# A DiT block on one core: the first K steps of the attention input by token tile, scalings by one engine each, plus-one on ScalarE, tile 2 normalized by VectorE

## The chip, the core and the metric

The kernel runs on one core of a Trainium2 chip. A core has a matrix engine (TensorE; in the profile PE, and PEld for its weight loads), VectorE (DVE), ScalarE (ACT), GpSimd (POOL) and SyncE (SP), which here only issues transfers. Each engine works through its own list of instructions in order; across engines an instruction waits on semaphores. The metric is the time of one execution on the device in microseconds (us); lower is better. Before and after are each the median of several runs.

## What is computed

One diffusion-transformer block on 2 x 256 tokens of width D = 1152, in bfloat16:

```python
mod = (_silu(c) @ w_mod).reshape(B, 6, 1, D)
shift_a, scale_a, gate_a, shift_m, scale_m, gate_m = [mod[:, i] for i in range(6)]
h = _layernorm(x, axis=-1) * (1 + scale_a) + shift_a
qkv = (h @ wqkv).reshape(B, N, 3, H, Dh)
...
a = jnp.einsum('bhqk,bkhd->bqhd', attn, v).reshape(B, N, D) @ wo
x = x + gate_a * a
h2 = _layernorm(x, axis=-1) * (1 + scale_m) + shift_m
m = _gelu(h2 @ w_fc1) @ w_fc2
return x + gate_m * m
```

The change lies entirely in the first two steps that use x: the layer norm with its scale, and the K part of `qkv`.

## The kernel before

The 512 tokens are four tiles of 128, numbered 0 to 3; tiles 0 and 1 belong to the first batch entry, 2 and 3 to the second. The width 1152 is nine chunks of 128, called k = 0 to 8. K, Q and V are then computed, followed by attention, the output projection, the second layer norm and the two feed-forward matrix products, all of which are untouched.

The start of the kernel, which the change reorders, works on several strands at once:

- **Statistics.** For tiles 0, 2 and 3 VectorE takes `bn_stats` of three pieces of 384 columns (line 167) and aggregates them (L169). Tile 1's sums come from two passes on ScalarE (L179), finished by three small VectorE operations (L184, L187, L190). ScalarE takes the square root (L195), VectorE the reciprocal (L198).
- **Normalization.** `norm1` writes the normalized tile `xn`, first its columns 0 to 511 (`CUT` is four chunks), later the rest. VectorE does it in one operation from mean and reciprocal (L211). ScalarE can do it too (L206), but then needs the product `nb` of mean and reciprocal (L200). Before, tile 2's first part is on ScalarE, all else on VectorE; `nb` is formed for tiles 0 and 2.
- **The scale.** `scale_group(g)` computes the scale for two or three chunks with 18 or 27 narrow matmuls from `w_scale_a` into a PSUM tile `pm` (L224), and VectorE adds one as it copies it to `scale_a` (L228).
- **Transposing and scaling.** `transpose_x` transposes 128 x 128 blocks of `xn` on TensorE into a PSUM tile `pt` (L234). `modulate` multiplies by the scale and writes the operand `hT0` (the profile calls it big), on VectorE (L241) or ScalarE (L243).
- **K steps.** `k_step(k, c0, c1)` multiplies chunk k of token columns c0 to c1 by six 128-wide weight blocks of `w_k` and adds into six PSUM banks `pk` that stay open over all k (L256). Each reloads the six weight blocks, however many columns it has.

What sets the order: the body is written out by hand, and the last lines of the kernel tie every instruction to the one recorded before it on its engine, so each engine runs exactly in the order of the source. The tiles `pc`, `pm` and `pt` share a pool named aux with two buffers, used in turn; a new one waits until the tile two before it has been read. Weights arrive through SyncE's queue in the fixed order of the source: a group of `w_scale_a`, then the rows of `w_k` for the same chunks, four times over; then the rest of `w_k`, `w_shift_a`, `w_q`, and so on. They are cut so that early chunks come first.

The order before: tile 0 and tile 1 are transposed for chunks 0 and 1 into one shared `pt_0`, the scale group comes between them, ScalarE scales chunk 0 for both tiles and VectorE chunk 1, and K steps 0 and 1 run over 256 token columns. Then tile 2 and tile 3 follow one at a time, with chunks 2 and 3 of the first two tiles in between. Each pair of chunks 2 and 3 is likewise shared between ScalarE and VectorE. A filler `warm(1)` of one matmul on zeros (L150) stands ahead of the first K step.

Of the kernel before, what the change touches and what calls it, by code (L numbers as in the profile page):

```python
# [8 lines left out]
FP32 = mybir.dt.float32  # L9
BF16 = mybir.dt.bfloat16  # L10
ACT = mybir.ActivationFunctionType
# [8 lines left out]
def kernel(  # L20
# [11 lines left out]
    nc = tc.nc  # L32
    B, N, D = x.shape
# [3 lines left out]
    P = 128  # L37
# [7 lines left out]
    NPD = D // PW  # L45
# [6 lines left out]
    const = ctx.enter_context(tc.tile_pool(name="const", bufs=1))  # L52
# [6 lines left out]
    def acc_tile(shape, name, dt=FP32):  # L59
        return psum.tile(shape, dt, name=name, tag="acc", bufs=6)  # L60

    def aux_tile(shape, name, dt=FP32):
        return psum.tile(shape, dt, name=name, tag="aux", bufs=2)
# [26 lines left out]
    make_identity(nc, ident[:])  # L90
    eps_t = const.tile([P, 1], FP32, name="eps_t")
    nc.vector.memset(eps_t[:], LN_EPS)  # L92
    SW = 32
    sT = act.tile([P, KD, SW], BF16, name="sT")
    nc.gpsimd.memset(sT[:], 0.0)
# [49 lines left out]
    pwarm = acc_tile([P, T], "pwarm")  # L145


    def warm(n, dst):
        for _ in range(n):
            nc.tensor.matmul(dst[:], zeros[:, 0:P], zeros[:], start=True, stop=True)  # L150
# [9 lines left out]
    mv1 = small.tile([P, NT, 2], FP32, name="mv1", tag="mv1", bufs=1)  # L160
# [2 lines left out]
    xns = [work.tile([P, D], BF16, name="xn", tag="xn", bufs=4) for _ in range(NT)]  # L163
    stats1 = [small.tile([P, NPD, 6], FP32, name="stats1", tag="stats1") for _ in range(NT)]

    def stats_piece(t, j):
        nc.vector.bn_stats(stats1[t][:, j, :], x_sb[:, t, j * PW:(j + 1) * PW])  # L167
        if j == NPD - 1:
            nc.vector.bn_aggr(mv1[:, t, :], stats1[t][:].rearrange("p a b -> p (a b)"))  # L169


    T_ACT = 1
# [10 lines left out]
    def act_stats_finish():  # L183
        nc.vector.scalar_tensor_tensor(  # L184
            dm2[:], dsum[:], -1.0 / (D * D), dsum[:], op0=ALU.mult, op1=ALU.mult
        )
        nc.vector.scalar_tensor_tensor(  # L187
            mv1[:, T_ACT, 1:2], dsq[:], 1.0 / D, dm2[:], op0=ALU.mult, op1=ALU.add
        )
        nc.vector.scalar_tensor_tensor(  # L190
            mv1[:, T_ACT, 0:1], dsum[:], -1.0 / D, pivot, op0=ALU.mult, op1=ALU.add
        )

    def sqrt1(t):
        nc.scalar.activation(rstd1[:, t:t + 1], mv1[:, t, 1:2], ACT.Sqrt, bias=eps_t[:], scale=1.0)  # L195

    def recip1(t, with_nb=False):
        nc.vector.reciprocal(rstd1[:, t:t + 1], rstd1[:, t:t + 1])  # L198
        if with_nb:
            nc.vector.scalar_tensor_tensor(  # L200
                nb1[:, t:t + 1], mv1[:, t, 0:1], -1.0, rstd1[:, t:t + 1], op0=ALU.mult, op1=ALU.mult
            )

    def norm1(t, c0, c1, eng):
        if eng == "a":
            nc.scalar.activation(  # L206
                xns[t][:, c0:c1], x_sb[:, t, c0:c1], ACT.Identity,
                bias=nb1[:, t:t + 1], scale=rstd1[:, t:t + 1],
            )
        else:  # L210
            nc.vector.tensor_scalar(  # L211
                xns[t][:, c0:c1], x_sb[:, t, c0:c1], mv1[:, t, 0:1], rstd1[:, t:t + 1],
                op0=ALU.subtract, op1=ALU.mult,
            )


    scale_a = act.tile([P, KD, B], FP32, name="scale_a")

    def scale_group(g):
        k0, k1 = KGROUPS[g]  # L220
        pm = aux_tile([P, k1 - k0, B], "pm")
        for j in range(k0, k1):
            for k in range(KD):
                nc.tensor.matmul(  # L224
                    pm[:, j - k0, :], w_scale_a[:, k, j * P:(j + 1) * P], sT[:, k, 0:B],
                    start=(k == 0), stop=(k == KD - 1),
                )
        return lambda: nc.vector.tensor_scalar_add(scale_a[:, k0:k1, :], pm[:], 1.0)  # L228

    def transpose_x(ks, ts, pt=None, js=None):  # L230
        pt = aux_tile([P, len(ks), len(ts) * P], "pt", BF16) if pt is None else pt
        for i, k in enumerate(ks):
            for j, t in enumerate(ts) if js is None else zip(js, ts):
                nc.tensor.transpose(pt[:, i, j * P:(j + 1) * P], xns[t][:, k * P:(k + 1) * P], ident[:])  # L234
        return pt

    def modulate(pt, i, k, t0, j0, w, eng):
        b = t0 // TPB
        dst, src, sc = hT0[:, k, t0 * P:t0 * P + w], pt[:, i, j0:j0 + w], scale_a[:, k, b:b + 1]
        if eng == "d":  # L240
            nc.vector.tensor_scalar_mul(dst, src, sc)  # L241
        else:
            nc.scalar.mul(dst, src, sc)  # L243

    def modulated_transpose(k):
        pt = transpose_x([k], range(NT))
        for b in range(B):
            modulate(pt, 0, k, b * TPB, b * N, N, "da"[k % 2])
# [3 lines left out]
    def k_step(k, c0=0, c1=T):  # L252
        for m in range(KM1):
            if k == 0 and c0 == 0:
                pk[m] = acc_tile([P, T], "pk")
            nc.tensor.matmul(  # L256
                pk[m][:, c0:c1], w_k[:, k, m * P:(m + 1) * P], hT0[:, k, c0:c1],
                start=(k == 0 and c0 == 0), stop=(k == KD - 1), skip_group_check=True,
            )
# [30 lines left out]
    CUT = 4 * P  # L290
    warm(16, pwarm)
    act_stats(ACT.Identity, dsum)
    for j in range(NPD):
        stats_piece(0, j)
    sqrt1(0)
    act_stats(ACT.Square, dsq)
    stats_piece(2, 0)
    recip1(0, True)
    norm1(0, 0, CUT, "d")
    stats_piece(2, 1)  # L300
    pt_0 = aux_tile([P, 2, N], "pt", BF16)
    transpose_x([0, 1], [0], pt_0, [0])
    act_stats_finish()
    sqrt1(T_ACT)
    stats_piece(2, 2)
    recip1(1)
    norm1(1, 0, CUT, "d")
    scale_group(0)()
    transpose_x([0, 1], [1], pt_0, [1])
    modulate(pt_0, 0, 0, 0, 0, N, "a")  # L310
    modulate(pt_0, 1, 1, 0, 0, N, "d")
    sqrt1(2)
    warm(1, pwarm)
    k_step(0, 0, N)
    k_step(1, 0, N)
    stats_piece(3, 0)
    recip1(2, True)
    norm1(2, 0, CUT, "a")
    stats_piece(3, 1)
    stats_piece(3, 2)  # L320
    pt_1 = transpose_x([0, 1], [2])
    for k in range(2):
        modulate(pt_1, k, k, 2, 0, P, "a")
    sqrt1(3)
    scale_group(1)()
    recip1(3)
    pt_2 = transpose_x([2, 3], [0, 1])
    modulate(pt_2, 0, 2, 0, 0, N, "a")
    modulate(pt_2, 1, 3, 0, 0, N, "d")
    norm1(3, 0, CUT, "d")  # L330
    k_step(0, N, N + P)
    k_step(1, N, N + P)
    pt_3 = transpose_x([0, 1], [3])
    for k in range(2):
        modulate(pt_3, k, k, 3, 0, P, "a")
    k_step(2, 0, N)
    k_step(3, 0, N)
    norm1(0, CUT, D, "d")
    norm1(1, CUT, D, "d")
    pt_4 = transpose_x([2, 3], [2, 3])  # L340
    modulate(pt_4, 0, 2, 2, 0, N, "a")
    modulate(pt_4, 1, 3, 2, 0, N, "d")
    norm1(2, CUT, D, "d")
    norm1(3, CUT, D, "d")
    k_step(0, N + P, T)
    k_step(1, N + P, T)
    scale_group(2)()
    k_step(2, N, T)
    modulated_transpose(4)
    k_step(3, N, T)  # L350
    modulated_transpose(5)
    k_step(4)
    scale_group(3)()
    modulated_transpose(6)
    k_step(5)
    modulated_transpose(7)
# [10 lines left out]
    def vec_section(stat, w, name):  # L367
        pn = aux_tile([P, CTW], "pn")
        for k in range(KD):
            wk4 = w[:, k, :].rearrange("p (j q r) -> p q j r", q=4, r=32)  # L370
            for i in range(4):
                nc.tensor.matmul(  # L372
                    pn[32 * i:32 * i + SW, :].rearrange("p (j r) -> p j r", r=32),
                    stat[:, k, :], wk4[:, i, :, :],
# [14 lines left out]
    for k in range(KD):  # L389
        for b in range(B):  # L390
            dst, src = hT[:, k, b * N:(b + 1) * N], hT0[:, k, b * N:(b + 1) * N]
# [37 lines left out]

    s_rows = work.tile([P, KD, SW], BF16, name="s_rows", tag="s_rows", bufs=1)  # L430
    nc.vector.transpose(s_rows[:].rearrange("p k c -> p (k c)"), sT[:].rearrange("p k c -> p (k c)"))
# [301 lines left out]
    for b in range(B):  # L733
        for m0 in range(0, MSPLIT, 2):
# [7 lines left out]
            nc.scalar.activation(gT[:, ms[0]:ms[-1] + 1, b * N:(b + 1) * N], pacc[:], ACT.Gelu_apprx_tanh)  # L742
    gcol = small.tile([P, SW], FP32, name="gcol", tag="gcol", bufs=1)
    nc.gpsimd.memset(gcol[:], 0.0)
    gcol16 = small.tile([P, SW], BF16, name="gcol16", tag="gcol16", bufs=1)
    grow16 = small.tile([P, SW], BF16, name="grow16", tag="grow16", bufs=1)

# [33 lines left out]
    for gi, (n, t, c0, cw) in enumerate(groups):  # L781
        b = t // TPB
        last = gi == len(groups) - 1
        pacc = acc_tile([P, cw], "pacc")
        for kk in range(KF):
            j, r = divmod(n * KF + kk, 27)
# [15 lines left out]
    for ins in list(nc.cur_bb.bb.instructions)[first_traced:]:  # L802
        eng = ins.engine
# [38 lines left out]
```

## Time and profile before

| what | value |
|---|---|
| median of three runs | 245.58 us (245.22 to 245.62) |
| the profiled execution's own time | 245.54 us |
| its span, first to last instruction | 243.7 us |
| granted TensorE clock, mean over the span | 0.997 of full |
| normalization of 512 columns on VectorE (L211), mean | 407 ns |
| the same on ScalarE (L206), mean | 812 ns |
| one `bn_stats` piece on VectorE (L167), mean | 549 ns |
| scaling 256 columns from PSUM on VectorE (L241), mean | 350 ns |
| scaling 256 columns on ScalarE (L243), mean | 474 ns |
| scaling 128 columns on ScalarE (L243), mean | 363 ns |

The means are those of the groups between 7 and 16 us. The profile is one execution; its times count from the first instruction of the span. An engine's busy time is the time its instructions take, whatever depends on them; a wait is put down to the instruction that ended it. TensorE overlaps its matmuls, so a matmul's own length (some 0.2 to 0.4 us) is more than its share of a stream: the distance from start to start is what it costs there. VectorE and ScalarE likewise overlap the ends of neighbouring instructions a little when the second does not wait for the first. A line such as `pt<-ident,xn` names the result and the operands.

### The profile page before, as it was taken

The page shows a single profiled execution, that of the slowest core. Times are in us where ns is not written, and L with a number is a line of the kernel's source. Part 1 is how long each engine was busy: PE and PEld are TensorE (multiplying, and loading weights), DVE is VectorE, ACT ScalarE, POOL GpSimd, SP SyncE. Part 2 cuts the span into 40 slices and gives each one's busy share as a digit, 9 for nine tenths or more (in the row PEclk, how much of TensorE's full clock was granted, in tenths as well). Part 3 has the DMA queues.
Part 4 walks back from the last instruction along what each step waited for, and adds up shares of the span by engine and source line. Part 5 has one row for each costly group of instructions (what it writes and reads, how often), then busy time and mean ns, then how long its engine had stood idle before and what let it go on. Part 6 is the DMA issues. An engine that isn't in the chain of part 4 may idle for free.

```text
span 243.7 us, 3933 instructions
## 1 busy us (share of the span) xinstructions
PE 236.2 (97%) x1659; PEld 141.3 (58%) x1668; DVE 84.2 (35%) x196; ACT 66.2 (27%) x129; POOL 31.4 (13%) x47
## 2 busy tenths in 40 slices
PE   7879999999999999999999999999999999999994
PEld 2476444465656675888744444444666666666673
DVE  2853541314644676820000089993010000000001
ACT  6542250233524074783332222333000000000000
POOL 1000004000310514400000000003122211111111
PEclk9999999999999999999999999999999999999998
DMA  6999999999989977779999999996920000000000
GB/s 226 328 333 360 384 349 324 359 354 342 346 199 346 344 208 185 193 187 332 327 337 191 233 298 329 328 327 181 310 96 16 19 16 16 16 21 29 18 19 16
DMA packets 69757, 53.89 MB, mean 221 GB/s; under 512 B 19035, under 2 KB 64363, under 8 KB 69739
## 3 DMA queue, kind: packets, MB, share of 16 engines
q1 hardware_dynamic: 69008, 52.43, 72.7%
q0 software_dynamic: 704, 1.20, 1.7%
q8 instruction: 13, 0.21, 0.4%
q14 instruction: 5, 0.04, 0.0%
q10 hardware_dynamic: 27, 0.00, 0.0%
HBM read 48.08 MB, written 1.19 MB: 202 GB/s over the span
## 4 chain that ended last, share of the span: by engine, by line
PE 93%; DVE 3%; DMA 2%; ACT 1%; issue 1%; DVEq 0%
PE pacc L787 29%; PE pacc L726 29%; PE pacc L628 7%; PE pacc L519 7%; PE pacc L446 5%; PE pk L256 4%; PE pk L285 2%; PE pacc L454 2%; DMA x_sb<-in_x_dram 2%; PE pn L372 1%; PE ps_s L474 1%; PE pa L546 1%; DVE stats L167 1%; PE pt L234 1%; PE pm L224 1%
## 5 line engine op out<-in xcount | busy, mean ns | idle before, releaser
L787 PE MATMUL pacc<-w_f,gT 128*128 128x384 bf16 (+2 forms) x468 | 70.5, 314 | 0.0
L726 PE MATMUL pacc<-hT,w_f 128*128 128x512 bf16 (+1 forms) x409 | 70.1, 332 | 0.3
L787 PEld LDWEIGHTS <-gT 128*128 128x128 bf16 x468 | 44.4, 98 | 26.3
L726 PEld LDWEIGHTS <-w_f 128*128 128x128 bf16 x414 | 40.5, 98 | 29.4
L437 DVE SCALAR_TENSOR_TENSOR late<-w_gate_mT,late 128x1152 bf16<-128x1152 bf16 x18 | 24.4, 1357 | 32.7 <-DMA w_gate_mT<-in_w_mod_dram 32.1
L793 DVE TENSOR_TENSOR tmp<-pacc,gate 128x384 f32<-128x384 f32 (+2 forms) x13 | 6.8, 526 | 67.0 <-PE pacc L787 54.8
L764 ACT ACTIVATE gT<-pacc 128x512 bf16<-128x512 f32 x26 | 15.5, 597 | 35.0 <-PE pacc L726 35.0
L795 POOL TENSOR_TENSOR o_sb<-tmp,x 128x384 bf16<-128x384 f32 (+1 forms) x12 | 11.7, 973 | 52.0 <-DVE tmp L793 52.0
L628 PE MATMUL pacc<-w_o,big 128*128 128x384 bf16 (+2 forms) x117 | 18.1, 314 | 0.0
L519 PE MATMUL pacc<-w_v,hT 128*128 128x384 bf16 x108 | 17.9, 326 | 0.0
L628 PEld LDWEIGHTS <-big 128*128 128x128 bf16 x117 | 10.9, 98 | 7.1 <-DVE big L273 0.6
L519 PEld LDWEIGHTS <-hT 128*128 128x128 bf16 x108 | 10.4, 98 | 7.2 <-issue 0.5
L256 PE MATMUL pk<-big,w_k 128*128 128x256 bf16 (+2 forms) x88 | 13.3, 292 | 0.5 <-ACT big L243 0.3
L634 POOL TENSOR_TENSOR x<-tmp,x_sb 128x384 f32<-128x384 f32 (+1 forms) x11 | 9.8, 888 | 19.4 <-DVE tmp L633 10.8
L446 PE MATMUL pacc<-hT,w_q 128*128 128x512 bf16 x53 | 11.8, 379 | 0.1
L428 POOL DMA_DIRECT2D gates_dram<-grow x4 | 2.0, 514 | 66.2 <-DVE grow L750 66.2
L256 PEld LDWEIGHTS <-w_k 128*128 128x128 bf16 x90 | 7.5, 98 | 3.6 <-issue 0.6
L446 PEld LDWEIGHTS <-w_q 128*128 128x128 bf16 x54 | 5.3, 97 | 6.4
L150 PE MATMUL pwarm<-zeros 128*128 128x512 bf16 x21 | 7.6, 524 | 1.2 <-DVE eps_t L92 1.2
L633 DVE TENSOR_TENSOR tmp<-pacc,gate 128x384 f32<-128x384 f32 (+2 forms) x13 | 6.7, 525 | 5.4 <-PE pacc L628 5.3
L742 ACT ACTIVATE gT<-pacc 128x512 bf16<-128x512 f32 x10 | 5.7, 595 | 7.0 <-PE pacc L726 7.0
L611 ACT ACTIVATE hT<-hT,shift_m,scale_m 128x256 bf16<-128x256 bf16 x12 | 6.2, 588 | 4.0 <-DMA hT<-xn 4.0
(98 smaller groups left out, 156.0 us busy)
## 6 DMA issues: line engine op xcount, KB each, us to landing
w_f<-in_w_fc_dram SPq DMA_DIRECT2D x14, 864.0 KB, 10.5
w_f<-in_w_fc_dram SPq DMA_DIRECT2D x2, 2592.0 KB, 10.7
w_f<-in_w_fc_dram SPq DMA_DIRECT2D x2, 1728.0 KB, 12.0
w_shift_a<-in_w_mod_dram SPq DMA_DIRECT2D x3, 864.0 KB, 10.6
w_v<-in_wqkv_dram SPq DMA_DIRECT2D x3, 864.0 KB, 11.3
w_gate_a<-in_w_mod_dram SPq DMA_DIRECT2D x3, 864.0 KB, 9.8
w_o<-in_wo_dram SPq DMA_DIRECT2D x3, 864.0 KB, 13.6
w_shift_m<-in_w_mod_dram SPq DMA_DIRECT2D x3, 864.0 KB, 9.8
```

What stands on the lines that cost most here:

```text
L150: nc.tensor.matmul(dst[:], zeros[:, 0:P], zeros[:], start=True, stop=True)
L256: nc.tensor.matmul(pk[m][:, c0:c1], w_k[:, k, m * P:(m + 1) * P], hT0[:, k, c0:c1], start=(k == 0 and c0 == 0), stop=(k == KD - 1), skip_g ...
L437: nc.vector.scalar_tensor_tensor(spill, wT[:, j, :], 1.0, s_all[:, b, :], op0=ALU.mult, op1=ALU.mult, accum_out=dst[:, b * KD + j:b * KD + ...
L446: nc.tensor.matmul(pq[m][:], w_q[:, k, m * P:(m + 1) * P], hT[:, k, :], start=(k == 0), stop=(k == KD - 1),)
L519: nc.tensor.matmul(pacc[:], hT[:, k, t * P:(t + 1) * P], w_v[:, k, pnl * PW:(pnl + 1) * PW], start=(k == 0), stop=(k == KD - 1),)
L628: nc.tensor.matmul(pacc[:], aT[:, k, t * P:(t + 1) * P], w_o[:, k, c0:c1], start=(k == 0), stop=(k == KD - 1),)
L634: (nc.vector if (t, i) in ((1, 2), (3, 3)) else nc.gpsimd).tensor_tensor(x1[:, t, c0:c1], tmp[:], x_sb[:, t, c0:c1], op=ALU.add)
L726: nc.tensor.matmul(dst, w_f1[m // KD][:, k, ml * P:(ml + 1) * P], hT[:, k, c0:c1], start=(k == 0), stop=(k == KD - 1),)
L764: nc.scalar.activation(gT[:, m, :], pacc[:], ACT.Gelu_apprx_tanh)
L787: nc.tensor.matmul(pacc[:], gT[:, kk, t * P:(t + 1) * P], w_f2[j][:, r, c0 - n * PW:c0 - n * PW + cw], start=(kk == 0), stop=(kk == KF - 1),)
L793: nc.vector.tensor_tensor(tmp[:], pacc[:], gate_m[:, b, c0:c0 + cw], op=ALU.mult)
L795: (nc.vector if last else nc.gpsimd).tensor_tensor(o_sb[:], tmp[:], x1[:, t, c0:c0 + cw], op=ALU.add)
```

## The change

Four things are done, all within the hand-written order of the start.

Tile 1 no longer shares `pt_0` with tile 0. Each is transposed into a PSUM tile of its own, scaled by one engine (tile 0 by ScalarE, tile 1 by VectorE), and K steps 0 and 1 run once over tile 0's 128 columns and once over tile 1's. The later pairs of chunks 2 and 3 are each scaled by ScalarE alone, and tile 3's chunks 0 and 1 by VectorE instead of ScalarE. The filler matmul is dropped.

For scale groups 0 and 1 ScalarE adds the one, with a constant `one_t` as the bias of an identity activation; groups 2 and 3 stay on VectorE.

Tile 2's first part is normalized by VectorE, and the two products `nb` are no longer formed.

The aggregation of tile 2's statistics moves behind the normalization of tile 1, and the plus-one of group 1 before tile 3's square root; tile 3's normalization now stands ahead of the transposes of chunks 2 and 3.

```diff
+    one_t = const.tile([P, 1], FP32, name="one_t")
+    nc.vector.memset(one_t[:], 1.0)
...
-    def stats_piece(t, j):
+    def stats_piece(t, j, aggregate=True):
         nc.vector.bn_stats(stats1[t][:, j, :], x_sb[:, t, j * PW:(j + 1) * PW])
-        if j == NPD - 1:
-            nc.vector.bn_aggr(mv1[:, t, :], stats1[t][:].rearrange("p a b -> p (a b)"))
+        if j == NPD - 1 and aggregate:
+            stats_aggregate(t)
+
+    def stats_aggregate(t):
+        nc.vector.bn_aggr(mv1[:, t, :], stats1[t][:].rearrange("p a b -> p (a b)"))
...
-        return lambda: nc.vector.tensor_scalar_add(scale_a[:, k0:k1, :], pm[:], 1.0)
+
+        def add_one(eng):
+            dst = scale_a[:, k0:k1, :]
+            if eng == "d":
+                nc.vector.tensor_scalar_add(dst, pm[:], 1.0)
+            else:
+                nc.scalar.activation(dst, pm[:], ACT.Identity, bias=one_t[:])
+
+        return add_one
...
-    recip1(0, True)
+    recip1(0)
     norm1(0, 0, CUT, "d")
     stats_piece(2, 1)
-    pt_0 = aux_tile([P, 2, N], "pt", BF16)
-    transpose_x([0, 1], [0], pt_0, [0])
+    pt_0 = transpose_x([0, 1], [0])
     act_stats_finish()
     sqrt1(T_ACT)
-    stats_piece(2, 2)
+    stats_piece(2, 2, False)
     recip1(1)
     norm1(1, 0, CUT, "d")
-    scale_group(0)()
-    transpose_x([0, 1], [1], pt_0, [1])
-    modulate(pt_0, 0, 0, 0, 0, N, "a")
-    modulate(pt_0, 1, 1, 0, 0, N, "d")
+    stats_aggregate(2)
+    scale_group(0)("a")
+    for k in range(2):
+        modulate(pt_0, k, k, 0, 0, P, "a")
+    pt_1 = transpose_x([0, 1], [1])
+    for k in range(2):
+        modulate(pt_1, k, k, 1, 0, P, "d")
     sqrt1(2)
-    warm(1, pwarm)
-    k_step(0, 0, N)
-    k_step(1, 0, N)
+    k_step(0, 0, P)
+    k_step(1, 0, P)
     stats_piece(3, 0)
-    recip1(2, True)
-    norm1(2, 0, CUT, "a")
+    recip1(2)
+    norm1(2, 0, CUT, "d")
+    k_step(0, P, N)
+    k_step(1, P, N)
     stats_piece(3, 1)
     stats_piece(3, 2)
-    pt_1 = transpose_x([0, 1], [2])
+    pt_2 = transpose_x([0, 1], [2])
     for k in range(2):
-        modulate(pt_1, k, k, 2, 0, P, "a")
+        modulate(pt_2, k, k, 2, 0, P, "a")
+    scale_group(1)("a")
     sqrt1(3)
-    scale_group(1)()
     recip1(3)
-    pt_2 = transpose_x([2, 3], [0, 1])
-    modulate(pt_2, 0, 2, 0, 0, N, "a")
-    modulate(pt_2, 1, 3, 0, 0, N, "d")
     norm1(3, 0, CUT, "d")
+    pt_3 = transpose_x([2, 3], [0, 1])
+    for i, k in enumerate((2, 3)):
+        modulate(pt_3, i, k, 0, 0, N, "a")
     k_step(0, N, N + P)
     k_step(1, N, N + P)
-    pt_3 = transpose_x([0, 1], [3])
+    pt_4 = transpose_x([0, 1], [3])
     for k in range(2):
-        modulate(pt_3, k, k, 3, 0, P, "a")
+        modulate(pt_4, k, k, 3, 0, P, "d")
     k_step(2, 0, N)
     k_step(3, 0, N)
     norm1(0, CUT, D, "d")
     norm1(1, CUT, D, "d")
-    pt_4 = transpose_x([2, 3], [2, 3])
-    modulate(pt_4, 0, 2, 2, 0, N, "a")
-    modulate(pt_4, 1, 3, 2, 0, N, "d")
+    pt_5 = transpose_x([2, 3], [2, 3])
+    for i, k in enumerate((2, 3)):
+        modulate(pt_5, i, k, 2, 0, N, "a")
...
-    scale_group(2)()
+    scale_group(2)("d")
...
-    scale_group(3)()
+    scale_group(3)("d")
```

## The prediction, made before the changed kernel was run

> **What bounds the kernel now.** I read the page first, then the chain that ended last, the busy times by stretch, the waits of TensorE, and last the timeline of the stretch that the diff touches.
>
> ```profile
> span 243.7 us, 3933 instructions
> ...
> PE 236.2 (97%) x1659; PEld 141.3 (58%) x1668; DVE 84.2 (35%) x196; ACT 66.2 (27%) x129; POOL 31.4 (13%) x47
> ...
> PE 93%; DVE 3%; DMA 2%; ACT 1%; issue 1%; DVEq 0%
> ```
>
> TensorE carries 93% of the chain. What is not TensorE must lie somewhere, and the stretches say where:
>
> ```profile
> 8.47:15.54 7.07, 4.87 (x76) 3.73 (x75) 4.76 (x19) 3.01 (x8) 0.00 (x0) 1.00 1.14 323
> 15.54:26.72 11.18, 11.07 (x129) 7.87 (x130) 3.48 (x13) 2.78 (x7) 0.00 (x0) 1.00 1.08 364
> 34.92:240.20 205.28, 204.93 (x1370) 123.30 (x1374) 67.66 (x142) 50.81 (x97) 30.39 (x40) 1.00 0.71 206
> ```
>
> Columns are the stretch, its length, busy time of PE, weight loads, VectorE, ScalarE, GpSimd, the granted clock and DMA. From 15.5 us to 240.2 us TensorE is gapless at full clock, so a microsecond saved before 15.5 us is saved at the end, unless a weight lands too late for it. Only 8.5 to 15.5 us has holes, and TensorE's waits name them:
>
> ```profile
> PE pt L234 <- DVE scale_a L228: 0.8, 2, 0.5
> PE pt L234 <- DVE xn L211: 0.6, 1, 0.6
> PE pt L234 <- ACT xn L206: 0.5, 1, 0.5
> PE pk L256 <- ACT big L243: 0.3, 1, 0.3
> ```
>
> The timeline there (start, length, what) gives the present dates and most prices:
>
> ```profile
> 8.73 0.60 PE L224 MATMUL pm<-sT,w_scale_a 128*128 128x2 bf16 x18
> ...
> 10.14 0.47 ACT L243 ACTIVATE big<-pt,scale_a 128x256 bf16<-128x256 bf16 x1 [1.41 <-PE pt L234]
> 10.51 0.28 ACT L195 ACTIVATE rstd<-mv,eps_t 128x1 f32<-128x1 f32 x1
> 10.65 0.35 DVE L241 TENSOR_SCALAR big<-pt,scale_a 128x256 bf16<-128x256 bf16 x1 [0.89 <-ACT big L243]
> ...
> 11.76 0.81 ACT L206 ACTIVATE xn<-x_sb,nb,rstd 128x512 bf16<-128x512 bf16 x1 [0.96 <-DVE nb L200]
> ...
> 12.95 0.62 ACT L243 ACTIVATE big<-pt,scale_a 128x128 bf16<-128x128 bf16 x2 [0.38 <-PE pt L234]
> ...
> 14.52 0.35 DVE L241 TENSOR_SCALAR big<-pt,scale_a 128x256 bf16<-128x256 bf16 x1 [0.57 <-ACT big L243]
> ...
> 15.25 0.29 PE L234 MATMUL pt<-ident,xn 128*128 128x128 bf16 x2 [0.60 <-DVE xn L211]
> ```
>
> To see there: VectorE's scaling waits for ScalarE to leave the shared pair (0.89 and 0.57 us), and the work queued behind it on VectorE, tile 3's normalization among it, waits too. Tile 2's normalization takes 0.81 us on ScalarE, against 0.41 us for the same shape on VectorE (L211).
>
> **What the Trainium skill says.** "PSUM — Partial Sum Buffer", PSUM bank collisions: two engines must not touch one bank at once, so their accesses are put in order. The trace agrees: those 0.89 and 0.57 us. "ScalarE: Activation LUTs", What ACT_TABLE_LOAD costs and Table sets: an ACTIVATE with a per-partition bias costs some 280 ns plus 0.83 ns an element, and cheap functions such as identity are in every table set. The trace agrees with the first (0.28 to 0.29 us for one element, L195); Identity already runs between Sqrts (L179, L206) with no table load between. "TensorE: Matmul & The Clock Gate", Part 1: the clock halves after an idle window of about 3.4 us. The trace has no such gap after the warm-up and a clock of 1.00 in all three stretches.
>
> **The change part by part.** TensorE's prices, start to start: four transposes 0.22 us (16.68 to 16.91), twelve 128-wide K matmuls 0.66 (16.91 to 17.57), eighteen scale matmuls 0.46 (17.57 to 18.03), six 256-wide 0.65 (18.03 to 18.68). A signal to another engine costs 0.03 to 0.05 us. I walk the new order with these.
>
> 1. VectorE's start. The two products nb (L200) go, 0.08 us each on the path (7.12 to 7.20), and tile 2's aggregation (0.23) moves behind tile 1's normalization, which starts at about 8.93 instead of 9.27 and ends at 9.34. I count this gain as nothing: see 2. The new memset of one_t (0.06) lies in VectorE's idle time before 4.81.
>
> 2. Scale group 0 and tile 0. The scale matmuls stay at 8.73 (they waited 0.15 us for w_scale_a) and end at 9.33. Plus-one on ScalarE: not in the trace; the page's price and the Sqrt row agree on 0.29 (VectorE's took 0.15; from above, 0.47, the 256-wide activation): 9.37 to 9.66. Two 128-wide activations, 0.62: 9.70 to 10.32. The "aux" tag has two PSUM buffers: tile 1's transposes now need a buffer of their own, and it is tile 0's, free only when ScalarE has read it. So they start at 10.37, later than the present 9.83, done 0.28 later. VectorE scales both chunks: one 256-wide takes 0.35, two 0.61, so 0.26 per 256 elements beyond a fixed 0.09; two of 128 come to about 0.35: 10.69 to 11.04. VectorE sits idle from 9.5 to 10.69, which is where part 1's gain goes.
>
> 3. K steps 0 and 1 as four half steps: 24 matmuls instead of 12 double ones, 1.32 us against 1.30. Tile 0's start behind the transposes at 10.48; tile 1's are due at 11.14, VectorE done at 11.04. They end at 11.80, against 11.97 before (10.67 plus 1.30). The warm-up matmul (0.21) went from a hole: nothing.
>
> 4. Tile 2. VectorE: first statistics of tile 3 (10.97 to 11.52), reciprocal (11.43 to 11.57; its Sqrt, on ScalarE behind tile 0's scaling, is done at 10.53), normalization 0.41: 11.61 to 12.02. Transposes at 12.07 instead of 12.62: 0.55 gained. Scale group 1 at 12.18; its weights land at 4.5 + 7.3 = 11.8. ScalarE scales tile 2 from 12.39 to 13.01, which frees the buffer for the transposes of chunks 2 and 3: 13.06 instead of 13.59. The plus-one follows (12.94 to 13.23).
>
> 5. Tile 3. VectorE pays 0.41 for tile 2 first, so the other statistics take 11.94 to 12.95 and the aggregation 13.22 (12.93 before). Sqrt 13.26 to 13.55, reciprocal to 13.74, then normalization directly, 13.78 to 14.19, not behind a scaling that waits for ScalarE (14.79 before). Transposes at 14.24 against 15.25: 1.01 gained, the largest piece.
>
> 6. What follows. ScalarE alone scales chunks 2 and 3 (0.84 for two, L243) from 13.49: done 13.96 and 14.33. K step 2 starts at 14.36 (15.37 before), K step 3 at 15.01 (16.01). Row 3 of w_k was issued at 7.57 (4.95 plus the queue's 2.57) and takes 7.4 to land: 14.97. Just in time; a larger gain would stop here. Then 15.66, 15.88, 16.54, 17.00 for the next transposes, tile 3's K steps, scale group 2 and K step 2's second half; ScalarE's two scalings of those transposes (16.07 to 16.91) are ready when used (17.00 and 17.87). From there the old order runs, 1.0 us earlier.
>
> 7. Later weights. w_scale_a's third group lands at 14.8 (due 16.5), the fourth at 18.5 (due 20.1); w_k's last rows by 20.7 (due about 24). w_shift_a's last third lands at 30.5 (18.7 plus 11.8), due about 31.4: 0.9 us to spare. w_q's first piece 32.1, due 33.7. The queue's order is unchanged.
>
> Sum: 1.0 us less. The profiled run took 245.54 us for a span of 243.7, and the median of the runs shown is 245.58: 245.54 - 1.0 = 244.5.
>
> **Rivals.** (a) The ScalarE chain of part 2 is longer. It starts from a transfer's landing at 8.7 and has no slack now: VectorE idles behind it. With the plus-one at 0.47, 0.1 us more for its own wait and a landing 0.2 later, parts 4 to 6 move by 0.5: 245.0. For it: every step is serial. Against: each price is a measured row. (b) Landings take over: with row 3 of w_k 0.9 us later, or the last third of w_shift_a 1.8, only 0.1 us of gain is left: 245.4. For it: w_k has no margin. Against: only row 3 is so near. Landings alone cannot end slower than before, since they would be waited for then too. (c) Slower: TensorE now idles once from 9.2 to 10.37. If the clock fell to half there, the 2.9 us of work until 13.9 (0.11 + 1.32 + 0.11 + 0.46 + 0.22 + 0.66) would take 5.8; the holes of some 0.9 us in that stretch absorb part, and about 2 us more remain: 246.5. It decides once the drop lasts for more than half of that. Against: 1.2 us is far under the stated window, and the trace's clock stood through holes of 0.5 us. (d) More: if landings come early and signals are at the short end, 1.4 us: 244.1.
>
> **How the numbers follow.** Forecast 244.5 with 0.66 (own range 244.1 to 245.0), (a) 0.16, (b) 0.06, (c) 0.06, (d) 0.06. The range 244.0 to 245.3 takes in (a), (d) and the two ends of the plus-one. 0.2%, about what can be told here, is 0.49 us, so the line is 245.09: the forecast, (d) and half of (a) are faster, 0.80; the rest of (a) and (b) are the same, 0.14; (c) slower, 0.06.
>
> **What would show it.** Right: transposes of tiles 1, 2 and 3 at about 10.4, 12.1 and 14.2; tile 1's later than before, the others earlier; K step 3 at 15.0; no hole after it. Wrong: a wait of K step 3 on w_k (b), a plus-one well over 0.3 us or VectorE idle beyond 10.7 (a), 128-wide K matmuls over 0.1 us apart (c).

## The result and the profile after

The changed kernel took 244.1 us (median of six runs, 243.66 to 244.63) beside 245.4 us for the kernel before (six runs, 245.16 to 246.8): a ratio of 0.994, interval 0.9913 to 0.9966. Two later repeats of the unedited changed kernel gave 0.9954 [0.9936, 0.9973] and 0.9935 [0.9907, 0.9963]. The forecast was 244.5 in a range of 244.0 to 245.3: the direction is right and the time lies in the range, 0.3 to 0.4 us under the forecast. Which step of the prediction failed is the question here.

One thing is needed to read sizes this small: in about a third of the runs of the kernel before (77 of the 229 for which it is recorded) the mean granted TensorE clock was 0.993 or less, and 61 of those took over 246.5 us, so each median below is also given for the runs at a clock of 0.997 or more (nothing lies between). On that footing the kernel before takes 245.16 us (152 runs; the middle half 245.12 to 245.34) and the changed one 244.12 (21 runs; 243.95 to 244.23): **1.04 us less**. The profile behind the prediction, at 245.54, sat 0.38 us above the kernel's usual time. The last section returns to the clock.

The page of the changed kernel, first its totals and then the shares of the chain of waits:

```profile
span 242.9 us, 3965 instructions
...
PE 237.0 (98%) x1679; PEld 141.6 (58%) x1679; DVE 84.3 (35%) x195; ACT 66.0 (27%) x131; POOL 31.4 (13%) x47
...
PE 86%; SPq 7%; DMA 5%; issue 0%; DVE 0%; DVEq 0%
```

The busy times of the engines barely move (TensorE's even shows 0.8 us more, with some of its records missing from the earlier profile); the span is 0.8 us shorter. Waits of TensorE in the same run, from 7 us on (us in total, times, longest):

```profile
PE pt L247 <- DVE mv L174: 0.5, 1, 0.5
PE pt L247 <- ACT big L256: 0.3, 1, 0.3
```

None of the four waits shown before is left in the list, and two smaller ones stand in their place. The transposes of tiles 2 and 3 still follow their normalization, but TensorE now stands for only about 0.1 us there. What that bought stands in the timeline of that run (start, length, what, and the idle time ahead with its releaser):

```profile
9.99 0.27 PE L247 MATMUL pt<-ident,xn 128*128 128x128 bf16 x2 [0.47 <-DVE mv L174]
...
11.89 0.28 PE L247 MATMUL pt<-ident,xn 128*128 128x128 bf16 x2
...
14.06 0.29 PE L247 MATMUL pt<-ident,xn 128*128 128x128 bf16 x2
14.18 1.47 PE L269 MATMUL pk<-big,w_k 128*128 128x256 bf16 x12
```

These lines are the transposes of tiles 1, 2 and 3 and the start of K step 2, due by the prediction at 10.37, 12.07, 14.24 and 14.36. All came earlier. Yet this is the slowest of the six runs: the second half of x landed at 6.9 us (6.2 in the profile before), VectorE ran late from there, and later a weight came late. The same stretch of a repeat of the same program that took 243.96 us is the better picture:

```profile
9.28 0.26 ACT L239 ACTIVATE scale_a<-pm,one_t 128x4 f32<-128x4 f32 x1 [0.75 <-PE pm L229]
9.57 0.63 ACT L256 ACTIVATE big<-pt,scale_a 128x128 bf16<-128x128 bf16 x2
9.59 0.27 PE L247 MATMUL pt<-ident,xn 128*128 128x128 bf16 x2 [0.35 <-ACT scale_a L239]
9.98 0.47 DVE L254 TENSOR_SCALAR big<-pt,scale_a 128x128 bf16<-128x128 bf16 x2 [0.58 <-ACT big L256]
...
11.48 0.28 PE L247 MATMUL pt<-ident,xn 128*128 128x128 bf16 x2
...
13.65 0.29 PE L247 MATMUL pt<-ident,xn 128*128 128x128 bf16 x2
13.78 1.47 PE L269 MATMUL pk<-big,w_k 128*128 128x256 bf16 x12
```

The third line is the one to look at. Tile 1's transposes start at 9.59, beside ScalarE's scaling of tile 0 (9.57 to 10.20) and not behind it; what released them was the plus-one. The prediction had them wait for that scaling.

### The profile page after: what moved, and what is told of

It is laid out like the page before. It is cut to its first block, busy times and chain, and to the rows that moved or that the text cites. A ratio compares the mean times of both kernels' runs of the same rounds, so it can differ in the third digit from the quotient of the medians.

```text
span 242.9 us, 3965 instructions
## 1 busy us (share of the span) xinstructions
PE 237.0 (98%) x1679; PEld 141.6 (58%) x1679; DVE 84.3 (35%) x195; ACT 66.0 (27%) x131; POOL 31.4 (13%) x47
## 4 chain that ended last, share of the span: by engine, by line
PE 86%; SPq 7%; DMA 5%; issue 0%; DVE 0%; DVEq 0%
PE pacc L803 29%; PE pacc L742 29%; PE pacc L644 7%; PE pacc L535 7%; DMA w_shift_a<-in_w_mod_dram 5%; PE pacc L462 5%; SPq L109 4%; PE pacc L470 2%; SPq L115 2%; PE pa L562 1%; PE ps_s L490 1%; PE pn L388 1%; PE pk L298 1%; SPq L104 1%; PE pg L422 0%
## 5 line engine op out<-in xcount | busy, mean ns | idle before, releaser
L269 PE MATMUL pk<-big,w_k 128*128 128x128 bf16 (+2 forms) x102 | 13.4, 278 | 0.0
```

Source lines behind the costliest of these rows:

```text
L269: nc.tensor.matmul(pk[m][:, c0:c1], w_k[:, k, m * P:(m + 1) * P], hT0[:, k, c0:c1], start=(k == 0 and c0 == 0), stop=(k == KD - 1), skip_g ...
```

## The experiments

Times are medians in us, with the number of runs; "clock up" means a mean granted clock of 0.997 or more. The ratio is to the kernel before on the same chip, over all runs. Differences below are between medians with the clock up: against 244.12 for edits of the changed kernel and against 245.16 for edits of the kernel before. They are good to some 0.1 to 0.4 us; the kernel before alone has 245.14 to 245.26 on the four chips.

| kernel | median | ratio, interval | median, clock up |
|---|---|---|---|
| before, again | 245.36 (18) | 0.9999 [0.9977, 1.0021] | 245.16 (10) |
| changed, repeats | 244.13 (11), 244.20 (9) | 0.9954 [0.9936, 0.9973], 0.9935 [0.9907, 0.9963] | 244.08 (8), 244.14 (7) |
| changed, tile 1 in tile 0's buffer | 244.95 (22) | 0.9988 [0.9966, 1.0011] | 244.71 (13) |
| changed, scale bank apart | 244.09 (9) | 0.9938 [0.9912, 0.9965] | 243.94 (6) |
| before, pair on ScalarE alone | 244.45 (22) | 0.9969 [0.995, 0.9988] | 244.41 (18) |
| before, tile 2 on VectorE | 244.57 (19) | 0.9949 [0.9932, 0.9966] | 244.57 (17) |
| changed, tile 2 on ScalarE | 244.40 (12) | 0.9965 [0.994, 0.9991] | 244.35 (11) |
| changed, plus-one on VectorE | 244.13 (14) | 0.9938 [0.992, 0.9957] | 244.12 (11) |
| changed, K steps not split | 244.48 (22) | 0.9965 [0.9948, 0.9982] | 244.31 (19) |
| changed, shift matmuls later | 244.17 (16) | 0.9952 [0.9934, 0.997] | 244.16 (13) |
| changed, tile 3 put later | 244.42 (18) | 0.9949 [0.9931, 0.9966] | 244.38 (14) |
| the same, scale bank apart | 244.37 (9) | 0.9939 [0.9915, 0.9963] | 244.37 (9) |
| changed, x tile 3 loaded later | 245.08 (22) | 0.9993 [0.9971, 1.0016] | 244.73 (11) |
| before, x tile 3 loaded later | 245.74 (14) | 1.0007 [0.9982, 1.0032] | 245.23 (8) |
| changed, the same, fewer fillers | 245.06 (22) | 0.9968 [0.9952, 0.9984] | 244.96 (18) |

**The two kernels again.** The changed kernel, unedited, and later the kernel before, unedited, give the noise and a second profile of each.

> The changed kernel once more, unedited, for a second profile. If the extra gain over the forecast comes from the order of the work (tile 1 transposed without waiting for ScalarE's scaling of tile 0), tile 1's transposes start again within 0.3 us of the plus-one's end and K step 4 begins about 1.2 us before the 19.78 us of before; if it came from transfers that happened to land early in the timed runs, the dates move by half a microsecond with the landings of x and of the scale weights. The shift weights' last third should land somewhere between 30.4 and 31.5 us; only where that is after about 31.2 should TensorE stand still there. Time 1.1 to 1.5 us below before.

> The kernel before, unedited, for a second profile beside the changed kernel's. Theory: VectorE's own order, not the landing of the first scale weights, paces it, so the start of K step 4 stands 19.3 to 19.8 us into the span and time is 245.1 to 245.6. Rival (the front follows the landing as in the changed kernel): tile 3's transposes start 6.5 us after the scale matmuls whatever their date.

> The changed kernel unedited on the same chip as the last three, as their measure. Theory: median 244.0 to 244.3 us, and in its profile tile 3's transposes 5.0 us after the start of the scale matmuls. Rival (that distance was chance): more than 0.3 us away from 5.0.

The changed kernel's transposes of tile 1 ran at 9.59 and 9.78 in its two repeats, never at the predicted 10.37. In both, tile 3's transposes came 5.0 us after the start of the first scale matmuls (8.64 to 13.65, 8.82 to 13.84), so there the start of the kernel follows these matmuls; in the kernel before the distance was 6.5 and 6.0 us. The second profile of the kernel before shows by how much the first one's base was late:

```profile
14.93 0.28 PE L234 MATMUL pt<-ident,xn 128*128 128x128 bf16 x2 [0.60 <-DVE xn L211]
...
19.46 1.46 PE L256 MATMUL pk<-big,w_k 128*128 128x512 bf16 x6
```

Tile 3 came at 14.93 where the prediction's base had 15.25, and K step 4 at 19.46 instead of 19.78: 0.32 us. In the earlier profile the first half of x landed at 4.7 us, here at 4.2.

**The assumed wait, put in.** The prediction says that tile 1's transposes need the PSUM buffer that tile 0 holds until ScalarE has read it. The edit makes this true:

```diff
-    pt_1 = transpose_x([0, 1], [1])
+    pt_1 = transpose_x([0, 1], [1], pt_0)
```

> Tile 1 is transposed into tile 0's own buffer, so that it waits for ScalarE's two scalings, as the prediction had assumed. Theory (the buffer was the error): tile 1's transposes start about 0.05 us after ScalarE's second scaling, some 0.4 to 0.5 us later than in the changed kernel; tile 2's and tile 3's transposes follow 0.3 to 0.5 us later, and the gain on before falls to 0.8 to 1.0 us. Rival (VectorE's normalizations set the pace anyway): tile 1 later by as much, but tile 3's transposes within 0.1 us of the changed kernel and the time equal to it.

It cost 0.6 us with the clock up (244.71 against 244.12) and 0.8 over all runs. What is left of the gain is 0.45 us, less than the 0.8 to 1.0 expected. The timeline:

```profile
10.61 0.27 PE L247 MATMUL pt<-ident,xn 128*128 128x128 bf16 x2 [1.01 <-ACT big L256]
10.72 2.33 PE L269 MATMUL pk<-big,w_k 128*128 128x128 bf16 x24
```

Here is the wait that was forecast, 1.01 us on ScalarE's scaling, so the unedited kernel doesn't have it. Why is seen in the placement of the built program: the tag "aux" does not hand out its two buffers in strict turn, as the description of the kernel before has it. Tile 0's transposes lie in PSUM bank 1, scale group 0 in bank 0, and tile 1's transposes in bank 0 again, which is free once the plus-one has read it. By what rule the bank is chosen is not shown. (The 2.33 us of the second line, 1.50 in the repeat, belongs to the clock, below; no profile of this kernel fell on a run with the clock up.)

The kernel before breaks the turn too. In strict turn its transposes of chunks 2 and 3 would take tile 2's buffer; they were placed in the bank of scale group 1. Its profile with x's last tile loaded later, an experiment below, tells the two apart:

```profile
12.69 0.63 ACT L245 ACTIVATE big<-pt,scale_a 128x128 bf16<-128x128 bf16 x2 [0.38 <-PE pt L236]
...
13.46 0.16 DVE L230 TENSOR_SCALAR scale_a<-pm 128x4 f32<-128x4 f32 x1 [0.79 <-PE pm L226]
...
13.68 0.38 PE L236 MATMUL pt<-ident,xn 128*128 128x128 bf16 x4 [0.25 <-DVE scale_a L230]
```

ScalarE has read tile 2 by 13.32, yet the transposes start only at 13.68, behind the plus-one. The same wait, at 13.59, is one of the two on `scale_a` in the profile that the prediction started from.

**That bank taken out of the pool.** If the scale group's results lie elsewhere, tile 1 doesn't even have to wait for the plus-one:

```diff
-        pm = aux_tile([P, k1 - k0, B], "pm")
+        pm = (acc_tile if g == 0 else aux_tile)([P, k1 - k0, B], "pm")
```

> The changed kernel with scale group 0's PSUM tile in a bank of the K steps, so that tile 1's transposes wait for its normalization alone and for no read of a buffer. Theory (the buffer still holds tile 1 by 0.2 to 0.3 us): tile 1's transposes start 0.05 to 0.1 us after its normalization, ahead of the plus-one's end, and time falls by 0.1 to 0.3 us below the changed kernel. Rival (the scaling waits for the plus-one anyway): VectorE's scaling of tile 1 still begins only after the plus-one, gain under 0.1 us.

With the clock up 243.94 against 244.12: 0.18 us less, which six runs do not settle (0.27 beside the kernel before on the same chip). The profile does not show what the edit is worth. Its scale weights landed early (matmuls at 8.16), the plus-one was over at 9.06, and tile 1's transposes waited for VectorE's normalization (8.92 to 9.33) and started at 9.48. There the bank would have been free in time without the edit.

**One edit of the change alone.** First the pair of chunks 2 and 3 scaled by ScalarE alone in the kernel before, then tile 2 normalized by VectorE in the kernel before:

```diff
-    modulate(pt_2, 1, 3, 0, 0, N, "d")
+    modulate(pt_2, 1, 3, 0, 0, N, "a")
```

> The kernel before with one edit: chunks 2 and 3 of tiles 0 and 1 are both scaled by ScalarE, so nothing of theirs stands ahead of tile 3's normalization on VectorE. Theory (the largest piece of the gain is the normalization of tile 3 released from that wait): tile 3's normalization starts at about 14.0 instead of 14.8 us, its transposes at 14.5 instead of 15.25, time 0.6 to 0.8 us below before. Rival (the gain needs the earlier tiles too): under 0.3 us.

```diff
-    recip1(2, True)
-    norm1(2, 0, CUT, "a")
+    recip1(2)
+    norm1(2, 0, CUT, "d")
```

> The kernel before with tile 2's first part normalized by VectorE, as in the change, and nothing else. Theory: tile 2's transposes come about 0.5 us earlier, but tile 3's still wait behind the shared scaling of chunks 2 and 3, so they move by no more than 0.3 us: time 0.1 to 0.3 us below before. Rival (this is the main piece): 0.5 us or more below.

Each alone brings most of the gain: with the clock up 0.75 us (244.41) and 0.59 us (244.57) against 245.16, together 1.34 where the whole change brings 1.04. They overlap. Transposes of tile 3, first with the pair on ScalarE:

```profile
13.72 1.12 DVE L211 TENSOR_SCALAR xn<-x_sb,mv,rstd 128x512 bf16<-128x512 bf16 x3
...
14.21 0.28 PE L234 MATMUL pt<-ident,xn 128*128 128x128 bf16 x2
```

then with tile 2 on VectorE:

```profile
13.56 0.35 DVE L241 TENSOR_SCALAR big<-pt,scale_a 128x256 bf16<-128x256 bf16 x1 [0.26 <-ACT big L243]
13.83 1.11 DVE L211 TENSOR_SCALAR xn<-x_sb,mv,rstd 128x512 bf16<-128x512 bf16 x3
...
14.29 0.28 PE L234 MATMUL pt<-ident,xn 128*128 128x128 bf16 x2 [0.60 <-DVE xn L211]
```

In the first, tile 3's normalization runs as soon as its reciprocal is there. In the second it still stands behind VectorE's scaling of the pair, but that scaling is itself early: it hangs on the transposes of chunks 2 and 3, and those on tile 2's, which came at 11.63 instead of 12.31. I had put the second edit alone at 0.3 us at most, as if only the queue behind the pair mattered; the miss shows that the pair was late because tile 2 was late.

**One edit of the change undone.** Tile 2 back on ScalarE; the plus-one back on VectorE; the first K steps whole:

```diff
-    recip1(2)
-    norm1(2, 0, CUT, "d")
+    recip1(2, True)
+    norm1(2, 0, CUT, "a")
```

> The changed kernel with tile 2's first part normalized by ScalarE again (and its product nb formed). Theory: the normalization costs 0.4 us more there, so tile 2's transposes come 0.5 to 0.6 us later, but VectorE, freed of 0.41 us, finishes tile 3's statistics that much earlier, so tile 3's transposes move by no more than 0.3 us either way: time 0.1 to 0.4 us above the changed kernel. Rival (tile 2 on VectorE is a main piece of the gain): 0.5 us or more above it.

```diff
-    scale_group(0)("a")
+    scale_group(0)("d")
...
-    scale_group(1)("a")
+    scale_group(1)("d")
```

> The changed kernel with the plus-one of scale groups 0 and 1 on VectorE again (0.15 us instead of 0.26). Theory: for group 0 VectorE has nothing else to do there, so tile 1's transposes start within 0.15 us of the changed kernel; for group 1 it stands behind tile 3's statistics or holds them up, which delays tile 3's transposes by 0.1 to 0.4 us: time 0 to 0.4 us above the changed kernel. Rival (the plus-one on ScalarE is what opened the path): 0.5 us or more above it.

```diff
-    k_step(0, 0, P)
-    k_step(1, 0, P)
+    k_step(0, 0, N)
+    k_step(1, 0, N)
...
-    k_step(0, P, N)
-    k_step(1, P, N)
```

> The changed kernel with K steps 0 and 1 over both tiles at once (256 columns), everything else as changed. Theory: the steps start about 0.4 us later, after VectorE's scaling of tile 1, so tile 2's transposes move by 0.2 to 0.4 us, but tile 3's, which wait for VectorE and ScalarE, by no more than 0.15: time 0 to 0.2 us above the changed kernel. Rival (the split carries the gain): 0.4 us or more above.

With the clock up they cost 0.23, 0.00 and 0.19 us. The changed kernel was not run again beside these three, and the kernel before was 0.10 us slower on their chip, so each may be 0.1 us too high. Tile 2 on VectorE is worth 0.1 to 0.2 where the pair is already on ScalarE and 0.59 where it isn't: the overlap again. No gain shows for the plus-one's move to ScalarE.

**Is a late weight the new bound?** In the changed kernel's own profile the chain ended in a transfer:

```profile
19.13 12.26 DMA w_shift_a<-in_w_mod_dram
31.43 0.55 PE pn L388 x12
```

The last third of w_shift_a landed at 31.39 and TensorE stood some 0.3 us for it, before the last twelve of these matmuls. If that bound the kernel as a rule, doing three rows of the last K panel first would fill the hole:

```diff
-    def k_panel(m):
-        pk[m] = acc_tile([P, T], "pk")
-        for k in range(KD):
+    def k_panel(m, k0=0, k1=KD):
+        if k0 == 0:
+            pk[m] = acc_tile([P, T], "pk")
+        for k in range(k0, k1):
...
+    k_panel(8, 0, 3)
     shift_a = vec_section(sT, w_shift_a, "shift_a")
-    k_panel(8)
+    k_panel(8, 3, KD)
```

> Three of the nine matmuls of K's last panel (8) go ahead of the shift section, so w_shift_a is needed 0.65 us later, at no added work. Theory (the shift weights' last third has become the bound in the changed kernel): no stand of TensorE in the shift section, the first Q matmul 0.2 to 0.4 us earlier than in a run of the changed kernel with the same landing, time 0.1 to 0.4 us below it and more even from run to run. Rival (landings are not the bound in most runs): the same time as the changed kernel, or up to 0.2 us slower because VectorE's shift now ends just as Q begins.

244.16 with the clock up: no gain. In the first repeat that weight landed at 30.7 and nothing waited for it. The edited kernel's own profile, a run of 245.04 us, stood 0.45 us for another late weight, the fourth scale group, which landed at 20.54. Such waits are real in single runs and not the kernel's bound.

**Two attempts to go further.** First, tile 2's normalization put ahead of tile 3's statistics, K steps 2 and 3 ahead of tile 3's transposes, scale group 2 ahead of tile 3's K steps; then the same with the scale bank apart:

```diff
-    stats_piece(3, 0)
     recip1(2)
     norm1(2, 0, CUT, "d")
+    stats_piece(3, 0)
...
+    k_step(2, 0, N)
+    k_step(3, 0, N)
     pt_4 = transpose_x([0, 1], [3])
...
-    k_step(2, 0, N)
-    k_step(3, 0, N)
...
+    scale_group(2)("d")
     k_step(0, N + P, T)
     k_step(1, N + P, T)
-    scale_group(2)("d")
```

> The changed kernel reordered: K steps 2 and 3 of the first two tiles go ahead of tile 3's transposes, tile 3's first statistics behind tile 2's normalization, scale group 2 ahead of tile 3's K steps. Theory (what is left of TensorE's stands is the wait for tile 3's normalization, and K steps 2 and 3 can fill it): K step 2 starts 0.2 to 0.6 us earlier, no stand at tile 3, time 0.2 to 0.5 us below the changed kernel. Rival (VectorE's scaling of tile 3 then comes too late, or row 3 of w_k has not landed): a new stand after the transposes of tile 3 or at K step 3, no gain.

> The last one with scale group 0's PSUM tile in a bank of the K steps besides. Theory: tile 1 is freed from the plus-one, and its gain of 0.1 to 0.2 us now adds, since the first statistics of tile 3 no longer stand between it and tile 2: 0.3 to 0.6 us below the changed kernel. Rival (the landing of the scale weights bounds both): equal to the last one within 0.1 us.

Both gave some 0.25 us away. Both made a new stand, for a bank that VectorE's scaling of tile 3 had still to read; in the first:

```profile
15.62 0.59 PE L229 MATMUL pm<-sT,w_scale_a 128*128 128x2 bf16 x18 [0.34 <-DVE big L254]
```

Second, the load of x's last tile (288 KB), needed only for statistics at about 11 us, issued behind the first scale weights so that these land earlier. This was done to both kernels, and to the changed one also with two of the sixteen filler matmuls less:

```diff
-    for b in range(B):
-        nc.sync.dma_start(x_sb[:, b * TPB:(b + 1) * TPB, :], x_v[:, b, :, :])
+    nc.sync.dma_start(x_sb[:, 0:2, :], x_v[:, 0, :, :])
+    nc.sync.dma_start(x_sb[:, 2, :], x_v[:, 1, 0, :])
...
+        if k0 == 0:
+            nc.sync.dma_start(x_sb[:, 3, :], x_v[:, 1, 1, :])
```

> The changed kernel with x's tile 3 (288 KB) loaded behind the first group of scale weights instead of ahead of it. Theory (the changed kernel's start follows the landing of the first scale weights, 5.0 us from there to tile 3's transposes in three profiles): the weights land 0.5 to 0.8 us earlier, tile 1's transposes come earlier until VectorE's normalization of tile 1 holds them, and time falls by 0.1 to 0.4 us. Rival (the fillers on TensorE or VectorE bound it as much): the scale matmuls still start at about 8.5 us, time equal to the changed kernel.

> The same edit on the kernel before. Theory (there VectorE and ScalarE pace the start, not that landing): time within 0.1 us of before, whatever the landing. Rival (the landing bounds both): as much faster as in the changed kernel.

> The changed kernel with x's tile 3 behind the scale weights, and 14 fillers on TensorE ahead of tile 0's transposes instead of 16. Theory: the scale matmuls start with the landing, at about 7.9 to 8.2 us, tile 1's transposes with its normalization (9.3), and time is 0.2 to 0.5 us below the changed kernel. Rival (fewer fillers let the clock come up late or fall again): a granted clock under full in the first 16 us and matmuls twice as long there, time above the changed kernel.

The first scale weights landed at 8.8 to 9.0 us in these three profiles, within the 8.1 to 9.1 of the fifteen without the edit, so the two fillers less brought nothing forward either (scale matmuls at 8.78). The second group landed at 12.6 to 12.8 instead of 11.2 to 12.1, and in the changed kernel TensorE stood for it:

```profile
12.72 0.60 PE L231 MATMUL pm<-sT,w_scale_a 128*128 128x2 bf16 x18 [0.70 <-DMA w_scale_a<-in_w_mod_dram]
```

With the clock up the edit cost the changed kernel 0.6 us (0.8 with fewer fillers) and the kernel before 0.07. So the change made the second group's landing matter: its plus-one now stands ahead of tile 3's square root on ScalarE, and tile 3's transposes came at 14.52 instead of 13.84. In the kernel before TensorE stood only 0.17 us for that weight. No version ran clearly faster than the changed kernel.

## Why the prediction was off, point by point

**Part 2, the buffer: this is the step that failed.** The prediction let tile 1's transposes wait until ScalarE had read tile 0's buffer, at 10.37. They start at 9.59 in the 243.96 us repeat. Of the 0.78 us, ScalarE's two scalings (9.57 to 10.20) show what the assumed wait would have given there, 10.25; so 0.66 is the buffer, and 0.12 the earlier scale weights (0.09) and a plus-one of 0.26 instead of 0.29. The experiment that puts the wait in costs 0.59 with the clock up, from the other side. The premise, two buffers in strict turn, was taken from the number of buffers and not from the bank that the program gives each tile.

**Part 2, VectorE's pair** was under-priced: 0.35 us for two 128-wide scalings out of PSUM, measured 0.47 to 0.48, and 0.07 more of start behind the transposes. That is the 0.20 us by which tile 3 gained less than tile 1: predicted 3.87 us between their transposes, measured 4.06 (9.59 to 13.65). So 0.78 - 0.20 = 0.58 us early at K step 4 (18.19 where 18.77 was due).

**The base** hid part of it. The profile it started from was 0.38 us over the kernel's usual time, 0.32 of it on the path at K step 4. The account with the clock up closes: what the change is worth with the assumed wait in it is 245.16 - 244.71 = 0.45 us; a late base adds 0.38 and the under-priced pair 0.20, which makes the forecast's 1.0. In truth the buffer adds 0.59 to the 0.45: 1.04. A forecast of 1.0 and a gain of 1.04 are near each other only because errors met: taken off the late base of 245.54, the missing 0.59 less the 0.20 of the pair is the 0.4 by which 244.5 lies over 244.12. Against that base the repeat moved K step 4 by 1.59 us (19.78 to 18.19).

**Part 1** counted VectorE's earlier start as nothing, because VectorE would idle behind ScalarE. With the buffer's wait gone that is no longer so: in the changed kernel's own profile it is VectorE, delayed by x, that tile 1 waits for (its normalization ended at 9.85; the wait is listed under the aggregation behind it, `mv`).

**Part 3** was right that the split costs little; undone, it loses 0.1 to 0.2 us, which the prediction did not claim. **Part 4 and part 5** were right in kind: tile 2 earlier through VectorE (0.1 to 0.6), and the pair on one engine, which frees tile 3's normalization, as the largest piece (0.75 alone). That the two overlap was in the walk, though no size for either alone was given.

**Part 6, the cap** on the gain from row 3 of w_k was wrong. K step 3 ran at 14.43 in the first repeat without a wait, though that row's landing was put at 14.97. The 7.4 us behind it belong to a neighbouring issue; no landing of row 3 itself is recorded in any of these traces. **Part 7** held, but for the 0.3 us stand on w_shift_a in one profile and the 0.45 us on the fourth scale group in another.

**The rivals.** (a), a longer ScalarE chain: no, the plus-one took 0.26. (b), landings: only in single runs. (d), more than forecast: nearest, but for another reason than early landings. (c), the clock: the hole that it named isn't there, so it could not decide. Its counter-argument, that a hole of 1.2 us is too short, fails all the same: with the assumed wait put in, TensorE's longest hole was 1.5 us and the clock fell. There it was 0.993 or less in 9 of 22 runs, five of them at 246.95 to 247.17: had the premise of part 2 held, (c) would have been worth more than its 0.06.

## What to carry to other kernels

Before a wait for a rotating buffer is put on the path, look up which bank each tile really gets, and who read that bank last: "two buffers" does not say in which turn. A wait in a trace can say the same: see whose end released the tile. Where a stretch is one serial chain, price the links from several profiles; a base that is 0.4 us off is as large as a step. And when two engines share a tile, ask both why the second one waits and why the first is late, since each cure alone can bring most of the gain.

## What the runs showed of the hardware

**The clock dropped after stretches with little matmul work, not only after idle ones.** The Trainium skill ("TensorE: Matmul & The Clock Gate", Part 1) speaks of an idle window of about 3.4 us. Two profiles show a drop without one. In each profile the record of the granted clock begins 4.4 to 7.4 us into the span, and every later change lies a whole number of 3.413 us after that (the first drop 2 and 3 times that in these two, 69 or 70 times in the others, at the very end), so the span falls into fixed stretches of that length. The kernel with tile 1 in tile 0's buffer, in two of them (length, busy time of PE, weight loads, VectorE, ScalarE, GpSimd, the granted clock, DMA share, GB/s):

```profile
7.78:11.19 3.41, 1.18 (x29) 1.12 (x30) 1.51 (x7) 1.37 (x5) 0.00 (x0) 1.00 1.13 330
11.19:14.60 3.41, 3.15 (x46) 3.09 (x44) 2.65 (x10) 0.96 (x4) 0.00 (x0) 0.50 1.15 321
```

and the kernel before with x's last tile loaded later, a run of 247.13 us:

```profile
11.84:15.25 3.41, 1.98 (x37) 1.53 (x36) 1.68 (x8) 1.76 (x5) 0.00 (x0) 1.00 1.15 321
15.25:18.67 3.42, 3.33 (x20) 2.59 (x21) 0.74 (x3) 0.63 (x2) 0.00 (x0) 0.50 1.10 342
```

TensorE was busy for 1.18 and 1.98 us of the first stretch and its longest holes were 1.5 and 0.6 us, and the next 3.41 us were granted half the clock. The matmuls of a K step pair show it:

```profile
15.52 2.77 PE L258 MATMUL pk<-big,w_k 128*128 128x256 bf16 x12
```

The same group takes 1.47 us at full clock. Busy time does not decide it, for two other stretches were followed by no drop, one in the changed kernel with K steps not split and one near the end of the kernel before with tile 2 on VectorE:

```profile
8.52:11.94 3.42, 2.13 (x32) 1.79 (x33) 2.43 (x10) 1.07 (x4) 0.00 (x0) 1.00 1.14 330
237.89:241.30 3.41, 1.51 (x28) 1.34 (x24) 0.62 (x3) 0.00 (x0) 0.73 (x1) 1.00 0.11 29
```

The last has 1.51 us of matmuls and kept the clock, where 1.98 lost it. What sorts these four is the work: the columns of all matmuls that start in the stretch, number times width. The two that lost the clock have 1444 (18 of 2 columns, 11 of 128) and 2340 (18 of 2, 18 of 128); the two that kept it 3364 (18 of 2, 2 of 128, 12 of 256) and 3072 (24 of 128). Counted so, all 1246 stretches at full clock in the eighteen profiles fall in line: the 20 with 2688 columns or fewer were followed by half the clock, all with 3072 or more kept it. Eighteen of the 20 lie at the kernels' ends, so only two bear on the time. At 56 ns for 128 columns, the distance of the last matmuls, the line lies at 34 to 39% of a full stretch. This comes from sorting the profiles; no run was made to try it, and some matmul records may be missing.

**Runs can be told apart by it.** One such window in 243 us takes 0.007 off the mean clock (half of 3.41 in 243). Runs of the kernel before at 0.993 or less lie mostly near 246.8 us, 1.65 over its others. Among 26 of the unedited changed kernel five have 0.993, at 244.81 to 245.03, 0.73 over its others. Why it loses less is not shown, since no profile fell on such a run of either unedited kernel; nor is it settled that it meets them less often, 5 of 26 against 77 of 229. It is part of why the ratios over all runs are better than 244.12 / 245.16 = 0.9958.

**A transfer moved behind another did not speed up the other.** With 288 KB less ahead of them the first scale weights landed at 8.8 to 9.0 us (8.1 to 9.1 without the edit), and the next group at 12.6 to 12.8 instead of 11.2 to 12.1.
